# Decayed attention and an ELU feed-forward layer on one core: later items in chunks of 64 consecutive tokens

## The chip, the cores and the metric

The kernel runs on one core of one Trainium2 chip. The metric is the device time of one execution in microseconds, as the median of several runs. TensorE (PE) multiplies matrices into PSUM, VectorE (DVE), ScalarE (ACT) and GpSimd (POOL) do the elementwise work, SyncE (SP) issues DMAs, and 16 DMA engines move the data. Each engine takes its instructions in the order of the program and waits at the head of its queue until what an instruction needs is there.

## What is computed

Attention without softmax: scores are weighted by a decay that depends on the distance of two tokens and is zero for later tokens. The result of all heads goes through a feed-forward layer (FFN) with an ELU.

```python
def _attn_ref(q, k, v):                      # (8, 8, 576, 64) each: batch, head, token, width
    scores = scale * np.matmul(q, k.transpose(0, 1, 3, 2))
    gamma = 1.0 - 2.0 ** (-5.0 - np.arange(H))
    rel = pos[:, None] - pos[None, :]
    Dmat = np.where(rel >= 0, gamma[:, None, None] ** rel[None, :, :], 0.0)
    return np.matmul(scores * Dmat[None], v)
...
x = attn_out.transpose(0, 2, 1, 3).reshape(4608, 512)
h = x @ w_in                                 # (512, 2048)
g = np.where(h > 0.0, h, np.exp(np.minimum(h, 0.0)) - 1.0)
return g @ w_out                             # (2048, 512)
```

## The kernel before

**Attention in chunks.** The decay is a product of a factor of the query's token and one of the key's token, so q and k are scaled by exponentials of their positions (`gq`, `gk`, L972), and what is left of the mask is ones and zeros. Within a chunk of tokens the scores are computed, masked and multiplied by v; all earlier chunks act through a running state, the sum of k times v, 64 x 64 for each head.

An item is 256 tokens of one batch and four heads: T is 0 or 1, the first or second 256 tokens, w the half of the heads. The 8 batches have 4 items each, n = 0 to 31; the last 64 tokens of all batches are two more tail items, t0 and t1. Items 0 to 4 are done piecewise (`early`), the others in joint steps.

- `load_main` (L363) loads q, k and v of an item by one DMA each from SP, 256 KB, with two neighbouring tokens on a partition: runs of 512 bytes in memory. The plan counts 0.9 us of transfer for each.
- `scaled` (L439) multiplies q and k with their factors, each in two halves e = 0, 1 (the even and the odd tokens), and `cast_v` (L475) turns v to bf16, all mostly on POOL. From item 7 on one DMA transpose from SP turns q and k (L530, 1.7 us in the plan); items before it are turned by PE (L491).
- A chunk is 128 tokens, c = 0 or 1, on 64 partitions in two halves of tokens. `do_scores` (L586) takes 16 matmuls of 64x64 weights and 128 columns into `sc`. Four such matmuls fill the four quarters of the array.
- `do_inter` (L611) adds what the running state gives: 2 matmuls of 128x128 weights and 128 columns for T = 0, 4 for T = 1.
- `do_values` (L631) takes 16 matmuls of 128 columns with the masked scores `pt`, and `do_state` (L653) 16 matmuls of 64 columns for the two chunks' states.
- `mask_step` (L721) multiplies `sc`, 128 x 1024, with the mask on DVE (L731). `after_state` (L667) adds up the states on DVE or ACT (`mid` L680, L678; `end` L687) and spreads each with zeros to 128x128 weights (`s_mid`, `s_end`, L695, mostly on POOL): two sums and two blocks for an item. `put_x` (L754) copies the result, transposed already, to the FFN's input `xt` (L766).

All matmuls are recorded at L256, in a helper. A joint step (`stretch`, L796) stands in PE's queue as inter-chunk of the previous item, scores of this one, values of the previous one, states of this one. It needs the mask and the blocks of the previous item and the turned q and k of this one.

**FFN.** Blocks of 256 tokens (the first six) or 512. `ffn1` (L859) multiplies `xt` with `w_in` in 128-row pieces, ACT and DVE make the ELU (L878 to L902), `ffn2` (L915) multiplies with `w_out` into an output tile of 128 rows, which ACT or DVE copies (L936) and SP stores (L944). Tiles named in `HALVED` (L206) are stored as two runs of 64 rows. `xt` has three buffers of 512 tokens, so attention can be at most three such blocks ahead.

**The order** is made by a planner in the kernel (`Plan`, L35). Each operation has a cost for each engine that may do it, a rank, buffers (`SLOTS`, L213) and operations that it waits for. The planner plays time forward and gives a free engine the ready operation of lowest rank; a DMA costs SP its issue and the wire its transfer time. The order that comes out is the program's order on each engine. In the first 50 us short matmuls on zeros are put where the plan has PE idle (L1036). So a cost in the plan changes no work, but where each piece stands in its queue.

Of the kernel before, what the change touches and what calls it, by code (L numbers as in the profile page):

```python
# [34 lines left out]
class Plan:  # L35
# [164 lines left out]
FROM = (8.9, 9.7, 10.5, 13.3, 16.6, 17.4, 18.2, 19.6)  # L200
ON = {}
DIRECT = True
AWAY = {("v", 0): 2.25}
TWO = False
LAST = (0, 256, 384, 512)
HALVED = ((10, 1), (10, 2), (12, 0), (12, 1), (12, 2))  # L206
ORDER = (0, 1, 2, 3, 4, 5, 6, 7, "t0", "t1")
PE_TURN = 7
WG = ("ck11", "ck11", "ck11", "ck12")
# [7 lines left out]
    "xt": 3, "g": 28, "e": 4, "em": 4, "ot": 5, "mid": 4, "end": 4, "s_mid": 4, "s_end": 18,  # L217
}


# [1 line left out]
def kernel(  # L222
# [70 lines left out]
    gq = const.tile([P, NU, H], FP32, name="gq")  # L293
    gk = const.tile([P, FT, H], FP32, name="gk")

    mask = const.tile([P, 2, 2, C], BF16, name="mask")
    nc.vector.memset(mask, 1.0)
    for c in range(2):
# [140 lines left out]
    def scaled(it, i, e, cost):  # L439
        n = it.n  # L440
        key, raw = ("qkn", n), ("rq" + "qk"[i], n)
        g = (gq, gk)[i][:, 2 * it.T + e, 4 * it.w : 4 * it.w + 4].unsqueeze(2).to_broadcast([P, 4, D])
# [7 lines left out]
        op = add(f"c{'qk'[i]}{e}{n}", cost, [it.ld["qk"[i]]], emit, it.rank,  # L450
                 take=[T("qkn", key, [P, 2, 2, 4, D], BF16)] if first else [], use=([] if first else [key]) + [raw],
                 after=it.cq0 if not first else None)
        if first:
            it.cq0 = op
        it.cq[i, e] = op
# [19 lines left out]
    def cast_v(it, cost):  # L475
        n = it.n

        def emit(op):
            pin(copy[op.eng](tiles["vn", n], tiles["rv", n]))  # L479

        it.cv = add(f"cv{n}", cost, [it.ld["v"]], emit, it.rank, take=[T("vn", ("vn", n), [P, 4, 2, D], BF16)],
                    use=[("rv", n)])

    def turn_pe(it, i, deps, src, key, dst_cls, n_of, cost):
# [21 lines left out]
    def prepare(it, turn):  # L506
        n = it.n
        if it.early:
            qc, kc = {"DVE": 0.44, "POOL": 0.62}, {"POOL": 0.62, "DVE": 0.44}
            vc = {"ACT": 0.62, "POOL": 0.65, "DVE": (0.42, 0.3)}  # L510
        else:
            qc = kc = {"POOL": 0.64, "DVE": (0.6, 1.5)}
            vc = {"POOL": 0.65, "ACT": (0.62, 1.0)}
        for i, c in ((0, qc), (1, kc)):
            if "qk"[i] in MERGE.get(n, ""):
                scaled_both(it, i, {"DVE": 0.69, "POOL": 1.2})
            else:
                for e in range(2):
                    scaled(it, i, e, c)
        cast_v(it, vc)  # L520
        it.turned = []
        if turn == "pe":
            cc = {"DVE": 0.42, "ACT": 0.59}
            for i in range(2):
                it.turned.append(turn_pe(it, i, [it.cq[i, 0], it.cq[i, 1]],
                                         lambda i=i: flat(n)[:, i * 512 : (i + 1) * 512], ("qkT", n), "qkT",
                                         (n, i), cc))
        else:
            def emit(op):
                pin(nc.sync.dma_start_transpose(tiles["qkT", n], flat(n)))  # L530

            it.turned.append(add(f"tr{n}", {"SP": 1.23}, list(it.cq.values()), emit, -1,
                                 take=[T("qkT", ("qkT", n), [P, 8, P], BF16)], use=[("qkn", n)], dma=(1.7, 64)))

    def prepare_tail(it):
        n = it.n
# [42 lines left out]
    def acc(key, bank, half, o, lhsT, rhs):  # L579
# [3 lines left out]
        seen |= halves  # L583
        mm(o, lhsT, rhs, start=first, stop=True, skip_group_check=True)

    def do_scores(it):  # L586
        n = it.n
        sc = tiles["sc", n]
        if it.tail:
# [21 lines left out]
    def do_inter(it, xkey):  # L611
        n = it.n
        if it.tail:
            for m in range(2):
                for j in range(2):
                    for hp in range(HP):
                        s = tiles["s_end", 4 * it.t + 2 * m + j, 1, hp // 2]
                        o = (m * HP + hp) * ST
                        acc((xkey, j), 0, 2, tiles[xkey, j][:, o : o + ST], s[:, hp % 2],
                            tiles["qkTt", n, m, j][:, hp, :ST])  # L620
            return
        for c in range(2):
            if it.T + c == 0:
# [7 lines left out]
    def do_values(it, xkey):  # L631
        n = it.n
        if it.tail:
# [8 lines left out]
                                tiles["vt", n, m][js, 2 * hp + i], pt[js, i, o : o + ST])  # L642
            return
        vn, pt = tiles["vn", n], tiles["pt", n]
        for hl in range(2):
            for e in range(2):
                for c in range(2):
# [5 lines left out]
    def do_state(it, views):  # L653
        n = it.n
        kn, vn = tiles["qkn", n], tiles["vn", n]
        for hl in range(2):
            for e in range(2):
                for c in range(2):
                    cs = slice(c * C, (c + 1) * C)
                    key, bank, ap = views[c]  # L660
                    for i in range(2):
                        acc(key, bank, i, ap()[i * D : (i + 1) * D, hl * D : (hl + 1) * D], kn[cs, 1, e, 2 * hl + i],
                            vn[cs, 2 * hl + i, e])

    total = {}
# [1 line left out]
    def after_state(it, st, views, bank_keys):  # L667

        n = it.n
        prev = total.get(it.w) if it.T else None  # L670

        def st_ap(c):
            return views[c][2]().rearrange("p (h d) -> p h d", h=2)
# [44 lines left out]
            it.bm = block(("mid", n), ("s_mid", it.b, it.T, it.w), f"bm{n}", mid)  # L718
        it.be = block(("end", n), ("s_end", it.b, it.T, it.w), f"be{n}", end)

    def mask_step(it, sc):  # L721
        n = it.n
        def emit(op):
            if it.tail:
# [3 lines left out]
                    mask_t.unsqueeze(1).to_broadcast([P, 4 * HP, ST]), ALU.mult,  # L728
                ))
                return  # L730
            pin(nc.vector.tensor_tensor(  # L731
                tiles["pt", n].rearrange("p i h n -> p (i h) n"),
                tiles["sc", n].rearrange("p i (h n) -> p (i h) n", h=2),
                mask.rearrange("p k e r -> p (k e r)").unsqueeze(1).to_broadcast([P, 4, 2 * P]), ALU.mult,
            ))

        it.mask = add(f"mask{n}", {"DVE": 1.22}, [sc], emit, it.rank + 1,
                      take=[T("pt", ("pt", n), [P, 2, 2, 2 * P], BF16)], use=[("sc", n)], banks=[("sc", 0)])

    def inter_deps(it):  # L740
        if it.tail:
            return [*it.cvs, *(at[4 * it.t + j, 1, w].be for j in range(4) for w in range(2))]
        return [it.cv, it.bm] + ([at[it.b, 0, it.w].be] if it.T else [])

    def inter_uses(it):
        if it.tail:
            return [("s_end", 4 * it.t + j, 1, w) for j in range(4) for w in range(2)] + [("pt", it.n)] + \
                [("qkTt", it.n, m, j) for m in range(2) for j in range(2)] + [("vt", it.n, m) for m in range(2)]
        return [("s_mid", it.b, it.T, it.w), ("qkT", it.n), ("vn", it.n), ("pt", it.n)] + (
            [("s_end", it.b, 0, it.w)] if it.T else [])  # L750

    xdone, xbegun = {}, set()
# [1 line left out]
    def put_x(it, xkey, dep):  # L754

        for c in range(2):
            def emit(op, c=c):
# [4 lines left out]
                else:  # L762
                    src = xs[:, : 2 * P].rearrange("p (h e r) -> p h e r", h=2, e=2)
                    o = it.T * TB + c * P
                    dst = xt[:, 2 * it.w : 2 * it.w + 2, o : o + P].rearrange("p h (r e) -> p h e r", e=2)
                    pin(copy[op.eng](dst, src))  # L766

            first = it.xt not in xbegun
# [5 lines left out]

    def cost_of(it, parts):
        t = 0.0
        if "i" in parts:
            t += 0.056 * (16 if it.tail else 6 if it.two else 4 if it.T else 2)
        if "s" in parts:
# [16 lines left out]
    def stretch(prev, it):  # L796
# [7 lines left out]
        if it is not None:  # L804
# [4 lines left out]
        views = [((xkey, c), 0, lambda c=c: tiles[xkey, c][:, 2 * P : 3 * P]) for c in range(2)]  # L809

        def emit(op):
            if prev is not None:
# [135 lines left out]

    for it in items:
        (load_tail if it.tail else load_main)(it)

# [126 lines left out]
```

## Time and profile before

| what | value |
|---|---|
| median of the runs (lowest to highest) | 306.41 us (306.09 to 307.36) |
| the profiled execution | 306.02 us |
| its span, first to last instruction | 303.8 us |
| granted TensorE clock | 1.00 |
| loads of q, k, v from SP (L375) | 95 of 256 KB; item 0's v is loaded from ACT |
| issue to landing of such a load, median | 5.0 to 5.4 us |
| DMA transposes of items (L530) | 25 |
| scalings on POOL (L445) | 121, 633 and 648 ns |
| blocks on POOL (L695) | 60, 615 and 633 ns |
| masks on DVE (L731) | 32, 1215 ns |
| SP's issues for the tail's loads (L403) | 24, 610 to 796 ns |

A line of the profile's groups names the source line, the engine and the operation, the tiles it writes and reads, how many there are, their busy time, the mean of one in ns, and how long the engine stood idle before them. A timeline line has the start, the busy time from the first start to the last end, and the number of instructions. Matmuls are pipelined: the next starts before the last has ended, so that the distance of starts is what a group costs PE.

### The profile page before, as it was taken

The page shows a single profiled execution, that of the slowest core. Times are in us where ns is not written, and L with a number is a line of the kernel's source. Part 1 is how long each engine was busy: PE and PEld are TensorE (multiplying, and loading weights), DVE is VectorE, ACT ScalarE, POOL GpSimd, SP SyncE. Part 2 cuts the span into 40 slices and gives each one's busy share as a digit, 9 for nine tenths or more (in the row PEclk, how much of TensorE's full clock was granted, in tenths as well). Part 3 has the DMA queues.
Part 4 walks back from the last instruction along what each step waited for, and adds up shares of the span by engine and source line. Part 5 has one row for each costly group of instructions (what it writes and reads, how often), then busy time and mean ns, then how long its engine had stood idle before and what let it go on. Part 6 is the DMA issues. An engine that isn't in the chain of part 4 may idle for free.

```text
span 303.8 us, 8244 instructions
## 1 busy us (share of the span) xinstructions
PE 294.5 (97%) x3281; PEld 171.0 (56%) x3323; DVE 210.1 (69%) x380; ACT 158.6 (52%) x309; POOL 148.3 (49%) x252
## 2 busy tenths in 40 slices
PE   7899999999999999999999999999999999999996
PEld 3688656758767775554554444555554444444445
DVE  3978935749888888788787666768766666666600
ACT  4548724738765554687653434466544343444311
POOL 5980389987999998988886324322000000000000
PEclk9999999999999999999999999999999999999999
DMA  7999999999999999999997767311111111011132
GB/s 213 266 206 211 233 294 325 224 305 267 222 278 210 257 202 306 249 240 243 232 252 188 173 154 159 79 37 37 37 33 38 36 36 35 35 37 36 35 103 72
DMA packets 103991, 50.08 MB, mean 165 GB/s; under 512 B 45841, under 2 KB 99473, under 8 KB 103953
## 3 DMA queue, kind: packets, MB, share of 16 engines
q1 hardware_dynamic: 99200, 45.10, 67.4%
q0 software_dynamic: 4224, 4.19, 8.3%
q8 instruction: 26, 0.43, 0.6%
q10 hardware_dynamic: 528, 0.26, 0.3%
q14 instruction: 13, 0.10, 0.1%
HBM read 36.70 MB, written 9.44 MB: 152 GB/s over the span
## 4 chain that ended last, share of the span: by engine, by line
PE 92%; DVE 3%; DMA 2%; issue 1%; POOL 0%; SPq 0%; ACT 0%; POOLq 0%; ACTq 0%
PE f L256 88%; PE sc L256 4%; DMA rqk<-in_k_dram 2%; DVE qkn L445 1%; DVE pt L731 1%; PE f L491 1%; DVE g L900 0%; DVE f L890 0%; POOL qkn L445 0%; DVE qkT L497 0%; DVE s_mid L709 0%; SPq L375 0%; DVE xt L766 0%; DVE end L687 0%; DVE s_end L695 0%
## 5 line engine op out<-in xcount | busy, mean ns | idle before, releaser
L256 PE MATMUL f<-xt,w_in_sb 128*128 128x256 bf16 (+1 forms) x754 | 142.9, 325 | 1.0 <-DVE xt L766 0.3
L256 PE MATMUL f<-w_out_sb,g 128*128 128x512 bf16 (+2 forms) x580 | 139.8, 368 | 2.4 <-issue 1.3
L878 ACT ACTIVATE e<-f 128x512 f32<-128x512 f32 x144 | 85.6, 597 | 91.0 <-PE f L256 86.5
L256 PEld LDWEIGHTS <-w_in_sb 128*128 128x128 bf16 x768 | 73.3, 98 | 51.8 <-DVE xt L766 0.6
L256 PEld LDWEIGHTS <-g 128*128 128x128 bf16 x608 | 56.6, 98 | 58.9
L892 DVE TENSOR_SCALAR em<-e 128x512 bf16<-128x512 f32 x90 | 44.5, 494 | 44.3 <-ACT e L878 43.8
L902 DVE SCALAR_TENSOR_TENSOR g<-f,em 128x512 bf16<-128x512 f32 x90 | 61.9, 689 | 7.1 <-DVE em L892 0.5
L731 DVE TENSOR_TENSOR pt<-sc,mask 128x1024 bf16<-128x1024 f32 x32 | 38.9, 1215 | 5.3 <-PE sc L256 5.3
L445 POOL TENSOR_TENSOR qkn<-rqk,gq 128x256 bf16<-128x256 f32 x59 | 37.5, 648 | 10.2 <-DMA rqk<-in_q_dram 10.2
L900 DVE SCALAR_TENSOR_TENSOR g<-e,f 128x512 bf16<-128x512 f32 x54 | 36.4, 683 | 8.0 <-ACT f L888 7.6
L445 POOL TENSOR_TENSOR qkn<-rqk,gk 128x256 bf16<-128x256 f32 x62 | 38.6, 633 | 3.6 <-DMA rqk<-in_k_dram 3.6
L936 ACT COPY ot<-f 128x512 f32<-128x512 f32 (+2 forms) x36 | 20.2, 563 | 20.3 <-PE f L256 14.6
L766 ACT CAST xt<-f 128x256 bf16<-128x256 f32 x50 | 20.1, 450 | 18.6 <-PE f L256 18.5
L695 POOL TENSOR_TENSOR s_mid<-mid,diag 128x256 bf16<-128x256 f32 x29 | 17.8, 615 | 23.8 <-ACT mid L678 12.5
L888 ACT ACTIVATE f<-f 128x512 f32<-128x512 f32 x48 | 28.4, 595 | 0.0
L695 POOL TENSOR_TENSOR s_end<-end,diag 128x256 bf16<-128x256 f32 x31 | 19.6, 633 | 5.4 <-DVE end L687 5.3
L479 POOL CAST vn<-rv 128x512 bf16<-128x512 f32 x29 | 18.6, 643 | 2.4 <-DMA rv<-in_v_dram 2.4
L546 POOL TENSOR_TENSOR qkt<-rqt,gq 128x256 bf16<-128x256 f32 x16 | 10.5, 677 | 15.3 <-DMA rqt<-in_k_dram 15.3
L256 PE MATMUL sc<-qkT 64*64 64x128 bf16 x512 | 13.4, 222 | 0.0
L256 PE MATMUL f<-pt,vn 64*64 64x128 bf16 x512 | 12.7, 217 | 0.4 <-DVE pt L731 0.4
L256 PEld LDWEIGHTS <-qkT 64*64 64x64 bf16 x512 | 8.2, 106 | 4.0 <-DVE qkT L497 0.6
L687 DVE TENSOR_TENSOR end<-f,mid 128x128 f32<-128x128 f32 x32 | 9.0, 283 | 1.2 <-ACT mid L678 0.3
(69 smaller groups left out, 135.2 us busy)
## 6 DMA issues: line engine op xcount, KB each, us to landing
rqk<-in_q_dram SPq DMA_DIRECT2D x32, 256.0 KB, 5.3
rqk<-in_k_dram SPq DMA_DIRECT2D x32, 256.0 KB, 5.4
rv<-in_v_dram SPq DMA_DIRECT2D x31, 256.0 KB, 5.0
out_dram<-ot SPq DMA_DIRECT2D x26, 256.0 KB, 2.9
out_dram<-ot SPq DMA_DIRECT2D x19, 128.0 KB, 2.3
w_in_sb<-in_moe_w_in_dram POOLq DMA_DIRECT2D x4, 512.0 KB, 9.2
w_out_sb<-in_moe_w_out_dram POOLq DMA_DIRECT2D x4, 512.0 KB, 14.9
rqt<-in_q_dram SPq DMA_DIRECT2D x8, 128.0 KB, 3.2
```

The source lines that it names most:

```text
L256: pin(nc.tensor.matmul(*a, **kw))
L445: pin(alu[op.eng].tensor_tensor(tiles[key][:, i, e], tiles[raw][:, :, e], g, ALU.mult))
L479: pin(copy[op.eng](tiles["vn", n], tiles["rv", n]))
L695: pin(alu[op.eng].tensor_tensor(tiles[key].rearrange("p h (j d) -> p h j d", j=2), tiles[src].unsqueeze(2).to_broadcast([P, 2, 2, D]), dia ...
L731: pin(nc.vector.tensor_tensor(tiles["pt", n].rearrange("p i h n -> p (i h) n"), tiles["sc", n].rearrange("p i (h n) -> p (i h) n", h=2), m ...
L766: pin(copy[op.eng](dst, src))
L878: pin(nc.scalar.activation(tiles[ekey], tiles[hkey], AF.Exp))
L888: pin(nc.scalar.activation(ph, ph, AF.Relu))
L892: pin(alu[op.eng].tensor_scalar_add(em, e, -1.0))
L900: pin(nc.vector.scalar_tensor_tensor(g, e, -1.0, ph, ALU.add, ALU.min))
L902: pin(nc.vector.scalar_tensor_tensor(g, ph, 0.0, tiles["em", blk, p], ALU.max, ALU.min))
L936: pin(copy[op.eng](tiles[okey][:, :cols], tiles[pkey][:, :cols]))
```

## The change

For the main items from n = 9 on (`FAR`), tokens p and p + 128 lie on partition p instead of 2p and 2p + 1. An item then has four chunks of 64 consecutive tokens, x = 0 to 3, chunk c = x % 2 by partition half and e = x // 2 by token half.

- q, k and v are each loaded by two DMAs, one for each e: 128 KB in runs of 256 bytes. The plan counts 0.62 us of transfer and 0.52 us of issue for each, and 1.9 us for a transpose.
- Scores and values keep their 16 matmuls, with 64 columns instead of 128; the mask works on 128 x 512. Inter-chunk takes 6 (T = 0) or 8 (T = 1) matmuls of 64 columns.
- There are four sums (on DVE, or the first on ACT) and four blocks for an item; the next step needs three of them. `mid` has 6 buffers instead of 4, `s_mid` 8 instead of 4.
- Factors for the other positions are made once: an iota on POOL, a cast and a product on DVE, two exponentials on ACT (planned from 22 us on).
- Eight output tiles are stored as two runs instead of five.

```diff
+FAR = 9
+FAR_LD = 0.62
+FAR_TR = 1.9
-HALVED = ((10, 1), (10, 2), (12, 0), (12, 1), (12, 2))
+HALVED = ((10, 0), (10, 1), (10, 2), (10, 3), (12, 0), (12, 1), (12, 2), (12, 3))
...
+        it.far = n >= FAR and not it.tail
...
+            if it.far:
+                for e in range(2):
+                    def emit_far(op, src=src, key=key, e=e):
+                        i0 = 2 * P * it.T + e * P
+                        pin(nc.sync.dma_start(tiles[key][:, :, e], src[it.b, 4 * it.w : 4 * it.w + 4, i0 : i0 + P, :].rearrange(
+                            "h p d -> p h d")))
+
+                    it.ld[s, e] = chain[0] = add(f"ld{s}{e}_{n}", {"SP": 0.52}, [], emit_far, len(plan.ops),
+                                                 take=[] if e else [T(cls, key, [P, 4, 2, D], FP32)],
+                                                 use=[key] if e else [], dma=(FAR_LD, 32), after=chain.get(0))
+                continue
...
+        if it.far:
+            for x in range(4):
+                for i in range(2):
+                    r = slice(i * D, (i + 1) * D)
+                    for c in range(2):
+                        cs = slice(c * C, (c + 1) * C)
+                        mm(sc[cs, i, x * C : (x + 1) * C], tt[r, 4 + x, cs], tt[r, x, cs], start=True, stop=True)
+            return
...
+            for x in range(4):
+                c, e = x % 2, x // 2
+                if it.T + x == 0:
+                    continue
+                s = tiles[("s_mid", it.b, it.T, it.w, x) if x else ("s_end", it.b, 0, it.w)]
+                for hl in range(2):
+                    acc((xkey, c), 0, 2, tiles[xkey, c][:, hl * P + e * C : hl * P + (e + 1) * C], s[:, hl],
+                        tt[:, e * 2 + hl, c * C : (c + 1) * C])
...
+            run = add(f"{key[0]}{x}_{n}", {"DVE": 0.29} if prev else {"DVE": 0.29, "ACT": (0.3, 0.2)},
+                      [st, prev and prev[0]], emit, it.rank + 2, take=[T(key[0], key, [P, 2, D], FP32)],
+                      use=[views[c][0]] + ([prev[1]] if prev else []), banks=[bank_keys[c]])
...
+            blk = add(f"b{x}_{n}", {"POOL": 0.62, "DVE": (0.42, 1.5)}, [run], emit_b, it.rank + 3,
+                      take=[T(name, out, [P, 2, P], BF16)], use=[key])
...
-        it.mask = add(f"mask{n}", {"DVE": 1.22}, [sc], emit, it.rank + 1,
+        it.mask = add(f"mask{n}", {"DVE": 0.69 if it.far else 1.22}, [sc], emit, it.rank + 1,
...
+        if it.far:
+            return ("i" in parts) * (0.27 + 0.06 * it.T) + 0.1 * sum(x in parts for x in "svt")
```

More of the change, by code (lines that the diff above doesn't have):

```diff
@@ L216 @@
     "rqt": 2, "rvt": 2, "qkt": 2, "vt": 4, "qkTt": 8,
-    "xt": 3, "g": 28, "e": 4, "em": 4, "ot": 5, "mid": 4, "end": 4, "s_mid": 4, "s_end": 18,
+    "xt": 3, "g": 28, "e": 4, "em": 4, "ot": 5, "mid": 6, "end": 4, "s_mid": 8, "s_end": 18,
 }
@@ L479, in emit @@
             pin(copy[op.eng](tiles["vn", n], tiles["rv", n]))
-        it.cv = add(f"cv{n}", cost, [it.ld["v"]], emit, it.rank, take=[T("vn", ("vn", n), [P, 4, 2, D], BF16)],
+        ready = [it.ld["v", 0], it.ld["v", 1]] if it.far else [it.ld["v"]]
+        it.cv = add(f"cv{n}", cost, ready, emit, it.rank, take=[T("vn", ("vn", n), [P, 4, 2, D], BF16)],
                     use=[("rv", n)])
@@ L532, in prepare @@
             it.turned.append(add(f"tr{n}", {"SP": 1.23}, list(it.cq.values()), emit, -1,
-                                 take=[T("qkT", ("qkT", n), [P, 8, P], BF16)], use=[("qkn", n)], dma=(1.7, 64)))
+                                 take=[T("qkT", ("qkT", n), [P, 8, P], BF16)], use=[("qkn", n)], dma=(FAR_TR if it.far else 1.7, 64)))
     def prepare_tail(it):
@@ L644, in do_values @@
         vn, pt = tiles["vn", n], tiles["pt", n]
+        if it.far:
+            pt = far_pt(n)
+            for hl in range(2):
+                for e in range(2):
+                    for c in range(2):
+                        cs = slice(c * C, (c + 1) * C)
+                        o = hl * P + e * C
+                        for i in range(2):
+                            acc((xkey, c), 0, i, tiles[xkey, c][i * D : (i + 1) * D, o : o + C], vn[cs, 2 * hl + i, e],
+                                pt[cs, 4 * i + 2 * e + hl])
+            return
         for hl in range(2):
@@ L748, in inter_uses @@
                 [("qkTt", it.n, m, j) for m in range(2) for j in range(2)] + [("vt", it.n, m) for m in range(2)]
-        return [("s_mid", it.b, it.T, it.w), ("qkT", it.n), ("vn", it.n), ("pt", it.n)] + (
+        mids = [("s_mid", it.b, it.T, it.w, x) for x in (1, 2, 3)] if it.far else [("s_mid", it.b, it.T, it.w)]
+        return [*mids, ("qkT", it.n), ("vn", it.n), ("pt", it.n)] + (
             [("s_end", it.b, 0, it.w)] if it.T else [])
@@ L808, in stretch @@
             cost += cost_of(it, "st")
-        views = [((xkey, c), 0, lambda c=c: tiles[xkey, c][:, 2 * P : 3 * P]) for c in range(2)]
+        views = [((xkey, c), 0, lambda c=c: tiles[xkey, c][:, 2 * P : 4 * P if it.far else 3 * P]) for c in range(2)]
         def emit(op):
@@ L947, in ffn2, with emit_far_i, emit_far_x, emit_far_f @@
                     dma=(0.67 * n / P * cols / DM, 8))
+    def emit_far_i(op):
+        pin(nc.gpsimd.iota(far_i, pattern=[[P, FT]], base=-MID, channel_multiplier=1))
+    def emit_far_x(op):
+        pin(nc.vector.tensor_copy(far_pos, far_i))
+        pin(nc.vector.tensor_tensor(far_expo, far_pos.unsqueeze(2).to_broadcast([P, FT, H]),
+                                    lgt.unsqueeze(1).to_broadcast([P, FT, H]), ALU.mult))
+    def emit_far_f(op):
+        pin(nc.scalar.activation(far_q, far_expo, AF.Exp, bias=bq))
+        pin(nc.scalar.activation(far_k, far_expo, AF.Exp, bias=bk, scale=-1.0))
+    far_ready = [add("far_i", {"POOL": 0.2}, [], emit_far_i, 0)]
+    for name, e, t, emit in (("far_x", "DVE", 0.45, emit_far_x), ("far_f", "ACT", 0.6, emit_far_f)):
+        far_ready[0] = add(name, {e: t}, [far_ready[0]], emit, 0)
+        far_ready[0].at = 22.0
     for it in items:
```

59 lines of the change are left out of this document (55 added, 4 removed).

## The prediction

> **What bounds the kernel now.** I read the page's busy shares and slices first, then the chain of waits in order of time, then PE's timeline around single attention steps, and last the groups of POOL and DVE and the issues of SP.
>
> ```profile
> span 303.8 us, 8244 instructions
> ...
> PE 294.5 (97%) x3281; PEld 171.0 (56%) x3323; DVE 210.1 (69%) x380; ACT 158.6 (52%) x309; POOL 148.3 (49%) x252
> ...
> PE   7899999999999999999999999999999999999996
> ...
> POOL 5980389987999998988886324322000000000000
> ...
> DMA  7999999999999999999997767311111111011132
> ```
>
> TensorE works from the second slice to the last, at a granted clock of 1.00. POOL and the DMA engines are full in slices 9 to 22, about 65 to 165 us, and nearly idle after. So attention (loads, scaling, turning, small matmuls) is made ahead of its use, the FFN is the rest of PE's queue, and the end is set by the sum of PE's work, as long as no attention step makes PE wait. PE's list of waits names 4.8 us in all, and none of its waits after the first 24 us is for attention.
>
> ```profile
> 69.19 0.35 PE sc L256 x16
> ...
> 153.32 0.35 PE sc L256 x16
> 153.67 0.67 PE f L256 x33
> 154.34 0.05 issue
> 154.39 10.74 PE f L256 x49
> ...
> 194.92 0.35 PE sc L256 x16
> ```
>
> Each item has one score group on the chain. The first line is item 9's, the second item 27's: 84.1 us for 18 items, 4.67 us each. Then comes 40 us of FFN alone until item 28. Attention is that far ahead.
>
> **What PE saves.** An attention step at 112.4 us (item 18's second half and item 19's first; both of T = 1, the second half of a batch) and the one for two tail groups, which already works in 64 columns:
>
> ```profile
> 112.38 0.28 PE L256 MATMUL f<-qkT,s_end 128*128 128x128 bf16 x2
> 112.49 0.28 PE L256 MATMUL f<-qkT,s_mid 128*128 128x128 bf16 x2
> 112.69 0.42 PE L256 MATMUL sc<-qkT 64*64 64x128 bf16 x16
> 112.94 0.39 PE L256 MATMUL f<-pt,vn 64*64 64x128 bf16 x16
> 113.17 0.29 PE L256 MATMUL f<-vn,qkn 64*64 64x64 bf16 x16
> 113.39 0.39 PE L256 MATMUL f<-xt,w_in_sb 128*128 128x512 bf16 x1
> ```
> ```profile
> 216.61 0.63 PE L256 MATMUL f<-qkTt,s_end 128*128 128x64 bf16 x16
> 217.17 0.45 PE L256 MATMUL sc<-qkTt 64*64 64x64 bf16 x32
> 217.44 0.44 PE L256 MATMUL f<-pt,vt 64*64 64x64 bf16 x32
> 217.81 0.39 PE L256 MATMUL f<-w_out_sb,g 128*128 128x512 bf16 x1
> ```
>
> Busy times overlap, so I go from start to start. In the step inter-chunk takes 0.31, scores 0.25, values 0.23, states 0.22: 1.01 us. With T = 0 (103.61 to 104.51) inter-chunk has two matmuls and takes 0.20: 0.90 us. In the tail step 16 inter-chunk matmuls of 64 columns take 0.56, 32 scores 0.27, and 32 values 0.37 with the hand-over to the FFN, 0.25 without.
>
> The program changes, over 23 items (11 of T = 0, 12 of T = 1): 16 scores and 16 values each go from 128 to 64 columns; inter-chunk goes from 2 or 4 matmuls of 128 columns to 6 or 8 of 64; states keep their 16. Half of the tail's 32 scores is 0.135 for 0.25, half of its values 0.125 for 0.22. Inter-chunk: the tail's 16 start 0.029 apart, with 0.13 to the next group, so 6 take 0.275 (0.20 before) and 8 take 0.33 (0.31). T = 0 saves 0.115 + 0.095 - 0.075 = 0.135, T = 1 saves 0.19. Sum: 11 x 0.135 + 12 x 0.19 = 3.8 us. By the spacing inside groups alone (scores 13.3 to 8.2 ns, values 11.9 to 8.1, 368 each; 70 matmuls at 55 ns out, 162 at 29 in) it is 1.9 + 1.4 - 0.85 = 2.5 us. I take 3.3, nearer to the tail's rows since they have the hand-overs in them.
>
> [...]
>
> **What the other engines get.** The changed program's order shows 69 loads becoming 138, still on SP; 46 more blocks on POOL or DVE; 46 more 128x128 adds on DVE.
> - DVE: 23 masks go from 1024 to 512 columns, 1.215 to about 0.69 (the 512-column g of 0.689 reads PSUM too): -12 us. 46 adds at 0.28: +13 us. The sum is nothing.
> - POOL: four scalings at 0.64, a cast at 0.64, four blocks at 0.62 or 0.63, 5.7 us an item for 4.5.
> - SP: six issues. The loads' median is 0.58, the tail's, of the same 512 runs of 256 bytes, 0.63; with gaps of 0.05, a transpose at 1.25 and most of a store: 5.0 to 5.8 us.
> - DMA: packets of 512 bytes mean 31.3 ns in the trace, those of 256 bytes in the tail stage (165 to 192 us, a lightly loaded one: share 0.71) 19. Loads queued one behind the other land 0.87 us apart. Two packets for one is 1.21 times that, 0.53 us for each half; by the commonest packets (27 and 18 ns) 0.58. An item's DMA work, 4.67 at most now, becomes 5.2 to 5.5.
>
> What may an item take? PE's order is fixed by the planner, so I counted the FFN matmuls that the two programs put between the score groups of items 9 and 27, at 0.2165 us for 512 columns and 0.1095 for 256. Before: 66.9 us, which with steps of 0.96 is 4.68 an item, and the trace shows 4.67. After: 94.6 us, with steps of 0.82, 6.08 an item. The slowest carrier needs 5.7, so PE should find its operands there. FFN work is at hand meanwhile: block 6 starts 12.3 us after the copy of item 15 (113.4 against 101.1), and 7 items at 1.4 more eat 9.8 of that. If that cover is gone, PE waits for every excess over 6.08.
>
> One wait is new: a step needs three blocks of the item before it, not one. After the states come three adds at 0.28 in a row, then a block at 0.62 behind at most a scaling of 0.64 on POOL, 2.1 us. The changed order has at least 4.3 us of FFN between two of these steps, and what is queued behind the wait on PE is FFN too.
>
> **The rest.** The 64-row stores move the same bytes: three more issues at 0.34 to 0.47 on SP in a stage where DMA is a tenth busy, nothing. Extra factors: an iota on POOL (0.13), a cast and a product on DVE (0.17 + 0.45), two exponentials on ACT (0.6). PE has 5.7 of 6 us busy there (18 to 24 us). They lie between zero and 0.6. The order in the first 20 us is reshuffled; its filler matmuls, which stand where PE would be idle, fall from 89 to 82 short ones, 0.4 us less. Not shown by any row is what the reshuffle does to a head that DVE paces: between -0.6 and +1.5 us, the latter being two of the 0.7 us scalings. I take +0.4 for all.
>
> **Sum.** 306.0 (execution: span 303.8 and 2.2 around it) - 3.3 + 0.4 = 303.1 us. The median of the runs shown is 306.4, so the profiled one is 0.4 below it.
>
> **Rivals.**
> - Short runs cost more than in the tail (slower). For: the tail is lightly loaded, and here every byte of 23 items moves in such runs, with stores and transposes between. Against: 282 packets of 256 bytes started in 0.25 us inside a transpose near 108 us, 0.45 us for 512. It decides from 0.67 us a half: (6.08 - 4.67 + 2.61) / 6. At 0.75 an item takes 6.56, 18 x 0.48 = 8.6 us on PE: 312 us. At 0.87, a half costing what a whole does now, 7.28: 18 x 1.2 = 21.6 us, 325 us. [...]
> - POOL is too slow. It would be 94% full. Its operations take 0.61 us, some 0.79. With half of them slow nine take 6.3 us: 18 x 0.22 = 4 us, 307 us. Against: the means used hold the slow ones already.
> - 64 columns take as long as 128, so that the change doesn't do what it says: no gain, and 92 x 0.055 = 5 us more, 311 us. The tail's rows speak against it.
> - The head loses 1.5 us more than I took: 304.6.
>
> **Chances.** Forecast (302.2 to 304.4) 0.64; short runs 0.14; POOL 0.11; columns 0.03; head 0.08. The range, 302.2 to 307.5, has the forecast, the head and most of POOL. Half a per cent is about what runs of 306.1 to 307.4 can tell from no change: faster than 304.9 has the forecast, half of the head and the mildest of POOL, 0.71; up to 307.9 the rest of these and the mildest of the short runs, 0.14; slower 0.15.
>
> **What would show it.** Scores of items 9 to 27 with 64x64 rows, about 0.135 us from start to start; steps of 0.77 and 0.82; 6.1 us an item; no `qkT`, `s_mid` or `pt` among PE's waits; POOL full to about 180 us. PE idle before scores with a transpose as releaser would mean the short runs, with s_mid as releaser POOL.

## The result and the profile after

The changed kernel takes 304.71 us (median of 22 runs, 303.89 to 306.56), the kernel before 306.10 us beside it (22 runs, 305.45 to 307.91). The ratio is 0.9955, with a 95% interval of 0.9942 to 0.9969: 1.4 us faster, where 3 us were forecast. Its profiled execution took 304.01 us, 2.0 us less than that of before.

The lines of its page that answer to those shown of before (span, busy times, and the slices of PE, POOL and the DMA engines):

```profile
span 302.0 us, 8622 instructions
...
PE 291.8 (97%) x3369; PEld 169.4 (56%) x3408; DVE 210.8 (70%) x428; ACT 158.1 (52%) x314; POOL 175.6 (58%) x296
...
PE   8999999999999999999999999999998999999996
...
POOL 4961289959899887998999995477740000000000
...
DMA  7999999999999999999999989757672111111132
```

PE is still full, but the 31st slice (226 to 234 us) has an 8. POOL and the DMA engines, at 0 to 3 tenths from 190 us on in the kernel before, now work at 4 to 7 tenths until about 225 us: their work reaches into the stage of the two tail items.

A step of the main items, as PE's timeline of the changed kernel shows it (start, busy time, group):

```profile
101.09 0.22 PE L259 MATMUL f<-qkT,s_end 128*128 128x64 bf16 x2
101.14 0.34 PE L259 MATMUL f<-qkT,s_mid 128*128 128x64 bf16 x6
101.41 0.32 PE L259 MATMUL sc<-qkT 64*64 64x64 bf16 x16
101.56 0.30 PE L259 MATMUL f<-pt,vn 64*64 64x64 bf16 x16
101.69 0.30 PE L259 MATMUL f<-vn,qkn 64*64 64x64 bf16 x16
101.92 1.05 PE L259 MATMUL f<-xt,w_in_sb 128*128 128x256 bf16 x8
```

From start to start: inter-chunk 0.32, scores 0.15, values 0.13, states 0.23, 0.83 us in all, where the step of before took 1.01. A step with T = 0 takes 0.77 (114.91 to 115.68) for 0.90.

The list of what PE waits for has two entries that the kernel before did not have, the second and the fourth of these (engine, line, what it waited for: us in total, times, longest):

```profile
PE f L516 <- DVE qkn L468: 1.0, 3, 0.4
PE sc L259 <- DMA qkTt<-qkt: 0.5, 1, 0.5
PE f L259 <- DVE xt L875: 0.4, 2, 0.2
PE f L259 <- POOL s_mid L805: 0.4, 1, 0.4
```

Both of these lie in the tail's two steps, as PE's timeline shows:

```profile
217.84 0.28 PE L259 MATMUL f<-qkT,s_mid 128*128 128x64 bf16 x4
218.49 0.23 PE L259 MATMUL f<-qkT,s_mid 128*128 128x64 bf16 x2 [0.37 <-POOL s_mid L805]
218.65 0.44 PE L259 MATMUL sc<-qkTt 64*64 64x64 bf16 x32
...
226.63 0.34 PE L259 MATMUL sc<-qkTt 64*64 64x64 bf16 x17
227.52 0.32 PE L259 MATMUL sc<-qkTt 64*64 64x64 bf16 x15 [0.55 <-DMA qkTt<-qkt]
227.65 0.44 PE L259 MATMUL f<-pt,vt 64*64 64x64 bf16 x32
```

Inter-chunk of item 31 takes 0.87 us (217.78 to 218.65) instead of 0.33: its last block comes late. The second tail item's scores take 1.02 us (226.63 to 227.65) instead of 0.27: the last transpose lands late.

**Where the microseconds went, by one sum.** PE never runs out of FFN work, so its time can be split: the FFN matmuls that the program puts between two points, at 0.2161 us for 512 columns and 0.1092 for 256, and the remainder, which is attention steps and waits. From item 9's first score to PE's end the remainder is 25.07 us before and 22.83 after, 2.24 less. Up to item 31's scores it falls from 21.18 to 17.93, by 3.25 us; from there on it rises from 3.88 to 4.90. The head, up to item 9, costs 0.36 us more (26.88 for 26.52). 3.25 - 1.02 - 0.36 = 1.87 us, and what lies around PE's work gives 0.14 more: the 2.0 us between the two profiled executions.

The profile shows how the tail comes late. Its chain of waits, in order of time (start, us, what), runs through the tail's loads from 207 us on, here from 210:

```profile
210.06 0.64 SPq L425
210.69 0.04 issue
210.74 4.46 DMA rqt<-in_k_dram
...
216.50 0.61 POOL s_mid L805
217.11 0.75 POOL vt L589
217.86 0.57 POOL s_mid L805
218.43 0.58 POOL s_end L805
...
220.46 1.18 SPq L425
221.64 0.04 issue
221.68 2.91 DMA rvt<-in_v_dram
...
225.03 2.45 DMA qkTt<-qkt
227.48 0.04 issue
227.52 0.32 PE sc L259 x15
```

The first of the two waits passes through POOL, whose timeline shows in what order its work stands:

```profile
212.43 1.18 POOL L571 TENSOR_TENSOR qkt<-rqt,gq 128x256 bf16<-128x256 f32 x2 [2.04 <-DMA rqt<-in_k_dram]
213.58 0.79 POOL L805 TENSOR_TENSOR s_mid<-mid,diag 128x256 bf16<-128x256 f32 x1
215.35 1.18 POOL L571 TENSOR_TENSOR qkt<-rqt,gq 128x256 bf16<-128x256 f32 x2 [0.98 <-DMA rqt<-in_k_dram]
216.50 0.61 POOL L805 TENSOR_TENSOR s_mid<-mid,diag 128x256 bf16<-128x256 f32 x1
217.05 0.81 POOL L589 CAST vt<-rvt 128x512 bf16<-128x512 f32 x1
217.82 0.61 POOL L805 TENSOR_TENSOR s_mid<-mid,diag 128x256 bf16<-128x256 f32 x1
```

The sums for the last two of these blocks of item 31 were ready on DVE at 213.23 and 214.10 us. The blocks started at 216.50 and 217.82, because tail scalings that waited for their load, and a tail cast, stand before them in POOL's queue. The second wait is the last transpose, at the end of SP's queue.

Most issues of a tail load (L425) occupy SP for 0.60 to 0.67 us and are followed by 0.05 of gap; the plan counts 0.46. With the plan's 0.8 on the wire, 1.25 before it and 0.55 behind it (in `Plan`), a load lands 2.6 us after its issue starts if nothing else is on the wire; in the trace it took 2.9 to 4.6, median 3.4. A tail transpose occupies SP for 1.25 us (1.23 in the plan) and lands 2.4 to 3.2 us after it starts, median 2.7; the plan's 1.0 on the wire makes that 2.8. So it is the loads that the plan has too cheap. Summed over its timeline, SP issues for 31.8 of the 37 us from 190 to 227, in the kernel before for 4.5: there the tail's eight transposes were issued from 163.9 to 191.5 us, here from 196.8 to 225.0.

### The profile page after: what moved, and what is told of

Its sections match the earlier page's. It is cut to its first block, busy times and chain, and to the rows that moved or that the text cites. A ratio compares the mean times of both kernels' runs of the same rounds, so it can differ in the third digit from the quotient of the medians.

```text
span 302.0 us, 8622 instructions
## 1 busy us (share of the span) xinstructions
PE 291.8 (97%) x3369; PEld 169.4 (56%) x3408; DVE 210.8 (70%) x428; ACT 158.1 (52%) x314; POOL 175.6 (58%) x296
## 4 chain that ended last, share of the span: by engine, by line
PE 79%; DMA 8%; POOL 7%; issue 2%; SPq 2%; DVE 1%; ACT 0%; POOLq 0%; ACTq 0%
PE f L259 76%; DMA rqk<-in_q_dram 5%; PE sc L259 2%; POOL qkn L468 2%; DMA rqt<-in_k_dram 1%; SPq L425 1%; POOL w_in_sb L446 1%; POOL w_out_sb L454 1%; POOL s_mid L805 1%; DMA rvt<-in_v_dram 1%; POOL qkt L571 1%; DMA qkTt<-qkt 1%; PE f L516 1%; POOL s_mid L756 0%; POOL s_end L805 0%
## 5 line engine op out<-in xcount | busy, mean ns | idle before, releaser
L989 ACT ACTIVATE e<-f 128x512 f32<-128x512 f32 x144 | 85.5, 597 | 87.5 <-PE f L259 85.2
L1003 DVE TENSOR_SCALAR em<-e 128x512 bf16<-128x512 f32 x90 | 47.3, 525 | 42.4 <-ACT e L989 41.6
L805 POOL TENSOR_TENSOR s_mid<-mid,diag 128x256 bf16<-128x256 f32 x69 | 42.8, 633 | 14.9 <-ACT mid L794 6.8
L468 POOL TENSOR_TENSOR qkn<-rqk,far_k 128x256 bf16<-128x256 f32 x46 | 29.8, 656 | 1.3 <-DMA rqk<-in_k_dram 1.3
L468 POOL TENSOR_TENSOR qkn<-rqk,far_q 128x256 bf16<-128x256 f32 x46 | 29.5, 660 | 0.4 <-DMA rqk<-in_q_dram 0.2
L468 POOL TENSOR_TENSOR qkn<-rqk,gq 128x256 bf16<-128x256 f32 x15 | 9.6, 650 | 14.3 <-DMA rqk<-in_q_dram 14.3
L830 DVE TENSOR_TENSOR pt<-sc,mask_t 128x512 bf16<-128x512 f32 x23 | 15.7, 681 | 0.0
L796 DVE TENSOR_TENSOR mid<-f,mid 128x128 f32<-128x128 f32 x46 | 13.1, 286 | 2.5
L805 POOL TENSOR_TENSOR s_end<-end,diag 128x256 bf16<-128x256 f32 x23 | 14.4, 626 | 0.5 <-DVE end L796 0.3
L836 DVE TENSOR_TENSOR pt<-sc,mask 128x1024 bf16<-128x1024 f32 x9 | 11.0, 1218 | 2.4 <-PE sc L259 2.4
L259 PE MATMUL sc<-qkT 64*64 64x64 bf16 (+1 forms) x512 | 11.1, 204 | 0.1
```

The costliest lines, as they stand in the source:

```text
L259: pin(nc.tensor.matmul(*a, **kw))
L805: pin(alu[op.eng].tensor_tensor(tiles[out].rearrange("p h (j d) -> p h j d", j=2), tiles[key].unsqueeze(2).to_broadcast([P, 2, 2, D]), dia ...
L830: pin(nc.vector.tensor_tensor(far_pt(n).rearrange("p (i x) n -> p i x n", i=2), tiles["sc", n][:, :, : 4 * C].rearrange("p i (x n) -> p i ...
L989: pin(nc.scalar.activation(tiles[ekey], tiles[hkey], AF.Exp))
L1003: pin(alu[op.eng].tensor_scalar_add(em, e, -1.0))
```

## The experiments

Every kernel was run beside runs of the kernel before; ratios are to those. The remainder is the sum of the section above, from item 9's first score to PE's end, of the profiled execution.

| kernel | median us | ratio (95%) | remainder us | of it from item 31 on |
|---|---|---|---|---|
| before | 306.10 | | 25.07 | 3.88 |
| after | 304.71 | 0.9955 (0.9942 to 0.9969) | 22.83 | 4.90 |
| e13_after_again | 305.00 | 0.9972 (0.9950 to 0.9995) | 23.51 | 5.10 |
| e1_five_stores | 305.02 | 0.9967 (0.9949 to 0.9984) | 22.81 | 4.88 |
| e3_tail_long_last | 305.22 | 0.9977 (0.9957 to 0.9998) | 21.55 | 3.61 |
| e4_before_tail_last | 308.27 | 1.0066 (1.0042 to 1.0090) | 25.07 | 3.85 |
| e5_old_loads | 304.93 | 0.9949 (0.9930 to 0.9968) | 22.76 | 3.62 |
| e9_loads_alone | 305.94 | 0.9990 (0.9981 to 0.9999) | 25.07 | 3.88 |
| e6_tail_as_measured | 303.60 | 0.9914 (0.9897 to 0.9932) | 22.09 | 3.62 |
| e7_measured_and_buffers | 302.52 | 0.9900 (0.9875 to 0.9924) | 21.55 | 3.62 |
| e11_both_again | 302.85 | 0.9904 (0.9868 to 0.9940) | 21.55 | 3.62 |
| e10_buffers_alone | 303.90 | 0.9914 (0.9892 to 0.9937) | 21.55 | 3.62 |
| e12_before_measured_buffers | 305.87 | 0.9988 (0.9971 to 1.0004) | 25.07 | 3.88 |
| e8_short_plan | 319.56 | 1.0406 (1.0377 to 1.0436) | 38.96 | 3.61 |

My theory after the result: PE's steps save what was forecast, and 1.3 us of it is lost because the tail items' operands come too late. Rivals: the stores in two runs cost it; the 256-byte loads cost it; the tail's place in the order costs it; the blocks of the new arithmetic cost it, through POOL alone.

### The stores

```diff
-HALVED = ((10, 0), (10, 1), (10, 2), (10, 3), (12, 0), (12, 1), (12, 2), (12, 3))
+HALVED = ((10, 1), (10, 2), (12, 0), (12, 1), (12, 2))
```

> The changed kernel with five tiles stored as two runs, as before, in place of eight. Theory A (PE loses 1.3 us in the two tail steps, at 217.8 and 226.6 us, because the tail's loads, scalings and transposes come too late): two of the three added stores, of tiles (10,0) and (10,3), are issued by SP inside that stage, at about 0.6 us each; without them the tail's last transpose can be at most 0.6 us earlier, so 304.7 falls by 0 to 0.6 us. Rival B (the missing 1.3 us are lost in the reshuffled first 60 us): no change, 304.7, since these stores come after 200 us.

Measured: 305.02 us, the tail's waits as they were.

```profile
PE sc L259 <- DMA qkTt<-qkt: 0.6, 1, 0.6
PE f L259 <- POOL s_mid L805: 0.3, 1, 0.3
```

The remainder is the same to 0.02 us. The stores are neither the loss nor a gain. (The profiled execution of this kernel is longer than after's because of its head, 28.57 for 26.88; more on that in the last section.)

### The tail at the end of the order

The tail's FFN block comes last, and its loads are planned with longer times; then the kernel before with the tail last.

```diff
-TAILS = 1
+TAILS = 0
...
-            chain[0] = add(name, {"SP": 0.46}, [], emit, len(plan.ops),
+            chain[0] = add(name, {"SP": 0.68}, [], emit, len(plan.ops),
...
-                           dma=(0.8, 32), after=chain.get(0))
+                           dma=(1.1, 32), after=chain.get(0))
...
-                                     dma=(1.0, 32)))
+                                     dma=(1.6, 32)))
```

> The changed kernel with the tail's FFN block as the last block instead of the last but one, and the tail's loads and transposes planned with the times seen in the changed kernel's trace (issue 0.68, transfers 1.1 and 1.6). Theory A (waits of the tail steps): PE has 27 us more of FFN before it needs the tail, both waits go, 304.7 - 1.3 = 303.4 us, and PE's waits name no s_mid and no qkTt. Rival B (loss in the first 60 us): 304.7, and item 9's scores stay at 66.0 us. Either way the end may cost some tenths, since the tail's last tile is stored in more, smaller runs.

> The kernel before with the tail's FFN block last: the control for the run with the tail last. Theory A: before has no wait in its tail steps, so the block's place is worth nothing there: 306.1 within 0.4. If it gains 1 us or more, the gain of the tail last in the changed kernel isn't that of the waits.

Measured: 305.22 and 308.27 us. With the tail last the two waits are gone, and the remainder falls to 21.55, 3.5 us under before. But what follows PE's last matmul grows from 2.8 to 4.96 us, in the control by the same amount (to 4.95); the stores at the end are more and smaller there (SP issues 13 from 284.7 us on, down to 32 KB, in the changed kernel 8, of 64 KB or more). So the control is 2.1 us slower than before, where 306.1 within 0.4 was expected, and e3 shows both things: without waits the change is worth 3.5 us on PE, and this place of the tail takes 2.15 back. The 303.4 us expected of e3 left this out, and its median alone would have hidden the gain.

### Loads of before with the new arithmetic, new loads with the arithmetic of before

The first keeps the chunks of 64 but loads q, k and v as before; the second is the kernel before with the split loads of 256-byte runs.

```diff
-            if it.far:
+            if False:
...
-                                 take=[T("qkT", ("qkT", n), [P, 8, P], BF16)], use=[("qkn", n)], dma=(FAR_TR if it.far else 1.7, 64)))
+                                 take=[T("qkT", ("qkT", n), [P, 8, P], BF16)], use=[("qkn", n)], dma=(1.7, 64)))
```

> The changed arithmetic with the loads of before: one DMA of 256 KB in runs of 512 bytes for each of q, k, v, planned at 0.9, transposes at 1.7. The loaded tokens are 2p and 2p+1 while factors, mask and output places are those of p and p+128, so the attention that it computes is another one; the work is the same. Theory A with the loads as cause: an item takes as long as POOL needs, 5.7 us, in place of 6.1, 18 items are 7 us ahead, the tail steps find their data: 303.4 us. Theory A with POOL's two more blocks as cause: the waits of the tail steps stay within 0.3 us, 304.4 to 304.7. Rival B (first 60 us): 304.7.

> The kernel before with one part of the change: q, k and v of items 9 to 31 are loaded by two DMAs each in runs of 256 bytes, planned as in the changed kernel; arithmetic, blocks, masks and stores are those of before. The loaded tokens are p and p+128 while the arithmetic takes them for 2p and 2p+1, so the attention that it computes is another one. If the longer loads cost nothing while FFN covers them (as the prediction has it): 306.1 within 0.5, with no wait for data beyond 0.3 us outside the tail steps. If the loads by themselves make the tail late: 306.6 to 307.4 with waits for qkTt.

For e9 the edit to the kernel before is the following (it also has the changed kernel's larger `mid` and `s_mid` buffers):

```diff
+FAR = 9
+FAR_LD = 0.62
+FAR_TR = 1.9
...
+        it.split = n >= FAR and not it.tail
+            if it.split:
+                for e in range(2):
...
+                        pin(nc.sync.dma_start(tiles[key][:, :, e], src[it.b, 4 * it.w : 4 * it.w + 4, i0 : i0 + P, :].rearrange(
+                            "h p d -> p h d")))
...
-                                 take=[T("qkT", ("qkT", n), [P, 8, P], BF16)], use=[("qkn", n)], dma=(1.7, 64)))
+                                 take=[T("qkT", ("qkT", n), [P, 8, P], BF16)], use=[("qkn", n)], dma=(FAR_TR if it.split else 1.7, 64)))
```

Measured: with the old loads 304.93 us, with the new loads alone 305.94. The loads alone cost PE nothing: remainder 25.07, and no attention wait in the list. The 23 items that e9 loads in runs of 256 bytes did not move the time by more than 0.2%. A doubled cost would have shown: a half of 0.87 us means 7.28 us an item, by the prediction's sum, and e9's items came at 5.97. A smaller cost can hide behind the FFN, and these runs do not exclude one: from 100 to 153 us the DMA engines of the kernel before move 251 GB/s at a share of 1.23 (this view's share can exceed 1), those of e9 204 at 1.01.

They do use up the slack, though. In e9 the tail's last transpose is issued at 224.1 us, where before has 191.5, and its scores start at 226.9: it just fits. In the changed kernel the same transpose is issued at 225.0 and the scores are placed at 226.6, and it does not fit. What it has more than e9 in this stage is POOL's work: 22.9 us busy from 190 to 227 us against 17.5. With the old loads the tail's steps are free of waits (3.62 us from item 31 on). So neither part alone makes PE wait in the two tail steps; both together do. The lead itself is spent by the loads: planned at their prices, they alone take the items from 4.67 to 5.97 us each. (e5 has 1.2 us of other waits, at three steps near 133, 139 and 205 us, with POOL's block as the one releaser that is named: near 205 us a tail cast stands before the block in POOL's queue, and PE's last two inter-chunk matmuls start at 205.21, after the block's end at 205.15. Its plan sets another pace, 5.57 us an item for 6.06 in after and 5.97 in e9. What held the other two steps is not settled. Its 304.93 us come nearest to the 304.4 to 304.7 expected with POOL's blocks as the cause, but the tail's waits that go with this are gone.)

### Planned transfer times

```diff
-FAR_LD = 0.62
-FAR_TR = 1.9
+FAR_LD = 0.45
+FAR_TR = 1.7
```

> The changed kernel planned with shorter transfers, 0.45 in place of 0.62 us for 128 KB in runs of 256 bytes, and 1.7 in place of 1.9 for a transpose. No work changes. If a half takes 0.53 us or more on the chip, as estimated from the tail's packets of the trace before, DMA needs 0.08 x 6 = 0.5 us an item more than planned where DMA sets the pace; over 18 items PE would wait up to 9 us, less where POOL's 5.7 us an item set the plan's pace anyway: 306 to 313 us. If a half takes 0.45, no waits: 303.5 to 304.7. This is the price of a half, which the range of the prediction was built on.

Measured: 319.56 us, beyond the 306 to 313 expected. It is the same work with shorter times in the plan; the list of waits:

```profile
PE sc L259 <- DMA qkT<-qkn: 5.5, 3, 3.6
PE f L259 <- POOL s_mid L805: 5.0, 8, 2.5
```

The plan then puts PE's steps before their operands are there. The waits are 10.5 us of the 17.4 us that the remainder grows over 21.55, and the granted clock takes another part. Soon after the longest wait (3.57 us, to 119.92) PE runs at half speed; the columns are the stretch, busy time and instructions of PE, PEld, DVE, ACT and POOL, the granted clock, the DMA share and GB/s:

```profile
121.30:124.70 3.40, 3.40 (x10) 1.19 (x9) 1.44 (x5) 1.17 (x3) 3.24 (x6) 0.51 0.91 202
125.00:131.00 6.00, 5.95 (x79) 3.08 (x79) 3.76 (x10) 3.51 (x7) 4.12 (x8) 1.00 1.01 215
```

A second such stretch, of 6.8 us at a granted clock of 0.5, starts at 216.9, after a wait of 2.5 us. By these clocks the 10.2 us cost about 5 us of work, an estimate; some 2 us of the 17.4 stay unassigned. So the longer transfer times in the diff are not decoration: without them the change would be a loss of 13 us.

### The tail planned as measured, and more buffers

If the tail's prices in the plan and its two buffers make it late, measured prices and four buffers should give the forecast's gain.

```diff
-    "rqt": 2, "rvt": 2, "qkt": 2, "vt": 4, "qkTt": 8,
+    "rqt": 4, "rvt": 2, "qkt": 4, "vt": 4, "qkTt": 8,
...
-            chain[0] = add(name, {"SP": 0.46}, [], emit, len(plan.ops),
+            chain[0] = add(name, {"SP": 0.68}, [], emit, len(plan.ops),
...
-                                     dma=(1.0, 32)))
+                                     dma=(1.3, 32)))
```

e6 has the last two edits alone, e10 the first alone, e7 and e11 all three; e12 is the kernel before with all three.

> The changed kernel in which only the plan of the tail's loads and transposes differs: SP issue 0.68 in place of 0.46 (0.63 and a gap of 0.05 in the trace) and transpose transfer 1.3 in place of 1.0. No work changes, only the order. Theory A1 (the plan puts the tail steps in PE's queue before their data can be there; other FFN work was at hand): the 0.5 and 0.7 us of waits go, 304.7 - 1.2 = 303.5 us. Rival A2 (the tail's data are late for the FFN itself, with nothing else to do): the wait moves to the start of the tail's FFN block and the time stays at 304.7.

> As the run with the tail planned as measured, and with four instead of two buffers for the tail's raw q and k and for their scaled form, so that a load need not wait for the scaling of the one two before it. Theory A1: the waits are gone already, so the same 303.5 us. Rival A2 (late for the FFN): the buffers let the tail's loads run ahead, and only this run of the two falls to 303.5.

> The changed kernel with rqt and qkt in four buffers instead of two, its plan as it was (issue 0.46, transpose 1.0). Theory A (the tail items come late because the plan prices their loads too low AND because two buffers let the next load start only when the old tile is used up): the buffers alone let the loads start earlier, so most of the 1.2 us at the two tail steps goes; 303.0 to 303.8 us, and no qkTt wait of over 0.2 us. Theory B (the price in the plan alone decides, the buffers are nothing): the qkTt and s_mid waits stay, 304.5 to 305. If it lies with the version that has both, the prices do nothing once the buffers are there.

> The version with the tail planned as measured and four buffers, run again beside the changed kernel and the two controls. Theory: 302.5 to 303.1 us, 1.5 to 2.2 below the changed kernel on the same chip, no attention wait on PE. If the earlier 302.52 was luck of few runs, it comes within 1 us of the changed kernel.

> Control: the kernel before with the same two edits (tail planned with 0.68 of issue and 1.3 of transpose, rqt and qkt in four buffers). PE's order is the same as before, only SP's order in the tail stage moves. Theory: before has no tail waits, so the edits give nothing, 305.8 to 306.4 us, and what the version with both gains over before (3.6 us) is the change's own. Rival: the edits are a gain of their own, of over 1 us, and the change is worth less than 2.5.

> The changed kernel unaltered, on the same chip as the three others. 304.2 to 305.0 us, ratio to before 0.994 to 0.997, with the qkTt and s_mid waits of 0.5 and 0.4 us. A second profile tells whether these waits and the tail steps' 1.0 us and 0.9 us come each time.

Measured: prices alone 303.60, buffers alone 303.90, both 302.52 and, run again, 302.85; the changed kernel on the same chip as the last 305.00, and before with the edits 305.87. Each of the two edits, prices and buffers, takes the tail's waits away, by another way. (Which of the two prices moved the order was not separated.) With the prices PE's order changes: the second tail item's scores are placed 2.9 us later (229.5 instead of 226.6), with FFN work in between, while its last transpose is issued later than before the edit (226.1). With the buffers the transposes come earlier (the last at 223.9). e6 still loses 0.54 us, nearly all of it at two steps near 97 and 102 us. The list of waits names nothing there, but the timelines do: the last two inter-chunk matmuls of these steps start at 96.64 and 101.98 us, 0.05 after POOL's last block ends (96.59 and 101.93). The list of waits of e11, the version with both, has no attention wait left:

```profile
PE f L259 <- DVE zero L264: 1.3, 1, 1.3
PE f L516 <- DVE qkn L468: 0.9, 3, 0.4
PE f L259 <- DVE xt L875: 0.4, 2, 0.2
```

and its chain at the place where after's ran through SP, POOL and the DMA engines is PE alone:

```profile
212.79 6.64 PE f L259 x68
219.43 0.38 PE sc L259 x32
219.81 9.34 PE f L259 x72
229.15 0.38 PE sc L259 x32
```

The control gains nothing that its interval can tell (0.9971 to 1.0004), so what e11 and e7 gain over before belongs to the change, once its tail is served: 3.3 and 3.7 us by the medians, 2.9 and 3.1 by the ratios. They beat both kernels. e10's median lies 1 us over e11's although its remainder is the same; its profiled execution has a head of 27.98 for 27.27, and two of its six runs a lower mean clock. What buffers without prices cost beyond that is open.

The second profile of the changed kernel (e13) has the tail's waits again, 0.8 and 0.3 us, and 0.5 us more at three earlier steps (near 97, 102 and 116 us). At the first and the last of these PE again starts just behind a POOL block (96.49 after 96.43, 115.80 after 115.75).

## Why the prediction was wrong

**PE's saving: right.** 3.3 us were taken, between 2.5 and 3.8. Where nothing waits, the remainder is 21.55 in four kernels (e3, e7, e10, e11) and 25.07 in four with the arithmetic of before: 3.52 us. Steps of 0.77 and 0.82 were forecast; 0.77 and 0.83 came. The upper end, start to start with the hand-overs, was the better one. Inter-chunk matmuls of 128 columns start 55 ns apart in the trace of before. With 64 columns, eight of them with weights of their own take 0.32 us here, 40 ns each with the hand-over.

**The head: near in size, by a guess.** +0.4 was taken, with no row behind most of it. The head is 26.88, and between 26.94 and 27.27 in e3, e6, e7, e11 and e13, against 26.52 to 26.77 in before, e4, e9 and e12; but e5 and e8, with other plans, have 26.71 and 26.73. From middle to middle that is some 0.3 us. In addition 5 of the 22 runs of the changed kernel, and 5 of 12 of e13, have a mean clock of 0.993 or 0.994, of before 5 of the 70 beside the experiments; without those five the median of the 22 would be 304.36 instead of 304.71. With e1, e5, e6, e7, e10 and e11, which have the new arithmetic, it is 27 of 81 runs; with e9 and e12, which have that of before, 5 of 94. (The kernels with the tail last have a lower clock at the end, and e8 has its long waits; they are left out.) In the profiles of e1 and e10, where it can be seen, the lower clock (0.5 for 3.4 us) lies in the head. No term of the sum had that, and it is part of why the medians differ by 1.4 us and the profiled executions by 2.0.

**Stores at nothing: right** (e1). **The loads' cost: right where it was asked.** Items 9 to 27 came at 6.06 us each, forecast 6.08, and PE waited for none of them in the profile of the changed kernel. The second one shows 0.5 us, of POOL's blocks.

**The step that failed** is "The slowest carrier needs 5.7, so PE should find its operands there". It weighed what SP, POOL and the DMA engines carry for an item against PE's pace, and took the end of the items for the end of the question. But the same queues carry the two tail items behind them, 24 loads and 8 transposes, on SP alone 24 x 0.68 + 8 x 1.30 = 26.7 us. In the kernel before they were served from 153.6 us on, far ahead of their use at 213 us; "POOL full to about 180 us" in the forecast already meant that this lead was being spent. In the changed kernel the first tail load is issued at 187.5 us and the last transpose at 225.0, for scores at 226.6. The row for it stood in the prediction (0.63 for a tail issue, with gaps of 0.05) and the plan's 0.46 stood in the code. Put against each other they would have asked whether the plan places the tail's steps too early. It does, by 0.54 us at the first of two steps and 0.75 at the second: 1.29 us over the 21.55 in the profile of after, 1.96 in e13 with the earlier steps. The prediction's sum had no term for it, and with the other measured terms it closes the account: 306.02 - 3.52 + 0.36 + 1.29 - 0.14 is 304.01, the profiled execution.

The same step failed in "behind at most a scaling of 0.64 on POOL, 2.1 us". At item 31 the last block started 3.7 us after its sum, behind two tail scalings, another block and a cast. And the 5.7 itself is not confirmed: e8's order leaves 5.68 us an item (87.5 us of FFN between the scores of items 9 and 27, and 18 steps of 0.82), and its items came at 6.24 with the waits. Which carrier held them is not separated; a transpose is named for 5.5 us of the waits, a POOL block for 5.0. In the changed kernel the order leaves 6.06, so this did no harm there.

**The rivals.** "Short runs cost more" did not come (e9), nor "64 columns as long as 128" (scores 0.15 us for 0.25, values 0.13 for 0.23). "POOL is too slow" came in a weak form that was not priced: not as a pace of 6.3 us an item, but as blocks and tail scalings that queue behind each other at the end, and in e6 and e13 as 0.5 us at single steps near 100 us. As the condition put it, s_mid as releaser meant POOL; it is one of the two new entries, the transposes the other. Both were looked for among items 9 to 27, and in the profile of the changed kernel they turned up behind them.

## What to carry to other kernels

A carrier that keeps pace with the work it feeds may still have used up the lead of whatever stands behind that work in its queue: count the queue to its last entry, and compare when that entry is done before and after. Where a planner fixes the order, compare its prices with the profile's rows for every kind of operation in the stage that fills up, since a price that was harmless in an idle stage (0.46 planned, 0.68 measured) can matter in a full one, as here, where the bounding engine waited 0.37 and 0.55 us. A split of time into fixed work and remainder, taken between the same two points in each kernel, tells gain and loss apart to a few hundredths of a microsecond where medians are a few tenths uncertain.

## What the runs showed of the hardware

PE's two longest waits in e8 were followed by a lower granted clock: the one of 3.57 us by 3.4 us at 0.51, the one of 2.5 us at 214.2 by 6.8 us at 0.5. In the heads of e1 and e10, too, 3.4 us at 0.5 (from 17.6 and 15.2 us) came after idle times of 0.9 and 0.5 us between short groups of matmuls; e7 has the 0.9 us alone and stays at 1.00. What brings the lower clock on is not shown by these runs. The heads of e1 and e10 are 28.57 and 27.98 us, the others' 26.5 to 27.3. The mean clock differs between runs of one program: it is 0.993 or 0.994 in 5 of the 22 runs of the changed kernel, 0.999 or 1.00 in the rest.

Runs of 256 bytes instead of 512, for 23 items of loads, cost the time nothing that shows (e9: 305.94 us, ratio 0.9990), though the page of e9 counts 140424 DMA packets where e12, with the loads of before, has 103990, and SP has 38 more issues between 60 and 190 us. Planned at their prices they did set the slower pace that brought the tail late: 5.97 us an item for 4.67. Whether SP's queue or the bytes would bind first is not shown: from 69 to 227 us SP issues for 0.80 to 0.89 of the time in e9, and from 69 to 175 us the DMA engines' share is 0.95 to 1.01.
